# Planned costs, due times and filler products changed in a hand-scheduled recurrence and two gated networks

## The chip, the cores and the metric

The kernel runs on one core of a Trainium2 chip. The metric is the device time of one execution in microseconds; lower is better. Three executions of the kernel before were timed.

## The reference

Three stages follow one another. A linear recurrence over 4 batches and 8 heads (768 positions, head size 48) keeps a 48x48 state for each batch and head; its output, 3072 tokens of 384 values, goes through a first network (d_ff 1536) and then a second (d_ff 2048):

```python
for t in range(S):
    state = alpha[:, :, t, :, None] * state + np.einsum('bhd,bhe->bhde', k[:, :, t], v[:, :, t])
    y[:, :, t] = np.einsum('bhd,bhde->bhe', q[:, :, t], state)
x = y.transpose(0, 2, 1, 3).reshape(B * S, H * D)
x = (x @ w_a) * (x @ w_b) @ w_out                                     # first network
h = x @ w_in
out = (np.maximum(h, 0.0) + alpha2 * np.minimum(h, 0.0)) @ w_out2     # second network
```

The weights arrive as float64; every matrix product is made from a high and a low part of each operand.

## The kernel before

**Work and its tiles.** The 3072 tokens are six blocks (0 to 5) of four chunks each, 24 chunks of 128 positions. A chunk loads `ra` (decay factors), `kq` (keys and queries) and `v` on SyncE's queue; VectorE scans the decays twice (L401, L411) and multiplies them into `kq` (L416); TensorE transposes the keys (`kps`, L452), makes `A` (L470), VectorE masks it to `As` (L479), TensorE makes `y` (L521 and after), and ScalarE and VectorE split `y` into the block's `x` (L605, L609). `A` and `y` of blocks 1 to 5 share one PSUM tile (`pair`), so `A` of a chunk waits until `y` of the chunk before it has been split. The `kq`, `ra` and `v` tiles are rings of two.

**The first network.** Its weights are 18 tiles: six units of `a`, `b` and `o`. Each is loaded as raw 64-bit words (L233) and converted by `conv` on VectorE and ScalarE (six VectorE instructions, L256 to L282). A step is one block with one half unit: nine products into `pa`, nine into `pb`, an elementwise product, and nine products into `acc` two steps later. There are 72 steps in the order of `SEGMENTS`: block 0 with units 0 and 1 (steps 0 to 3), block 1 with units 0 and 1 (steps 4 to 7), the same two blocks with units 2 and 3 and then 4 and 5, and from step 24 on blocks 2 to 5 with all units, 12 steps each. The `pa` and `pb` products keep this order strictly.

**The planner.** No order is written by hand. `Graph.run` is a list scheduler: each operation has an engine, a planned duration, a planned extra latency `lat`, a key and its dependencies; whichever engine can start earliest takes, among its operations that the plan holds ready, the one with the smallest key. The order that results is fixed in each engine's queue, and each engine then runs its queue strictly in that order. Keys are planned nanoseconds. Step k is due at

```python
at = [T_MOE + int(k * 27 * MM * STRETCH) for k in range(len(flat) + LAG + 1)]
```

with MM = 228, and `block_at[n]` is the due time of the first step of block n. A chunk's operations have a key before `block_at[n]`, its loads a key still earlier (`early`); a conversion has the due time of its unit less a lead, its load 15000 less than that. The elementwise operations of a step have keys 40000 before it.

**Filler products.** Where the plan sees TensorE idle by more than PAUSE, `fill` (L176 to L184) puts products of a small constant tile into the queue (`wp`), one for every 110 ns of seven tenths of the planned gap. Their results are used nowhere. They are instructions of the queue: they run whether or not TensorE would in fact have been idle.

**Moves.** In blocks 2 to 5, six small SyncE transfers (L625) bring part of `x` to other partitions before the first `pa` of that block.

Of the kernel before, what the change touches and what calls it, by code (L numbers as in the profile page):

```python
# [23 lines left out]
BC = 4  # L24
# [10 lines left out]

MM = 228
HOP = 250
T_MOE = 32000
STRETCH = 1.22
URGENT = 40000  # L40
PAUSE = 500
SLACK = 1000


class Op:
# [93 lines left out]
def body(tc, akq, v, vg, w_a, w_b, w_o1, w_in, w_o2, beta, out):  # L139
# [13 lines left out]
    with ExitStack() as ctx:  # L153
# [22 lines left out]

        def fill(t0, t1):
            t = mpool.free()
            if t is None or t > t0 + 100:
                return  # L180
            mpool.log.append([])
            wp = ps_mm.tile([P, MB // 2], F32, name="wp", tag="mm")
            for _ in range(int((t1 - t0) * 0.7) // 110):
                nc.tensor.matmul(wp, warm[:, 0:P], warm, start=True, stop=True)  # L184
# [16 lines left out]
        for t in range(KT):  # L201
            for i in range(2):
# [3 lines left out]
                )  # L206

        G = Graph(fill)
        units, uses = {}, {}


        flat = [(n, i, s) for s, (n, u0, u1) in enumerate(SEGMENTS) for i in range(2 * u0, 2 * u1)]
        at = [T_MOE + int(k * 27 * MM * STRETCH) for k in range(len(flat) + LAG + 1)]
        due, block_at = {}, {}
# [8 lines left out]
        def conv(src, tag, name, key, wait, sink, early=15000, on_pe=False, halves=None):  # L223
# [8 lines left out]
                b["raw"] = wpool.tile([P, UC], I64, name=f"r{name}", tag=tags[0])  # L232
                nc.sync.dma_start(b["raw"], src)  # L233

            ld = G.add("SP", 2000, load, key - early, wait, 4000)
            free = cring.take()
            last, highs = [], []
            for n in range(2 if halves else 1):
# [48 lines left out]
                x = G.add("DVE", d(550), sign, key, [m])  # L287
                x = G.add("DVE", d(930), main, key, [x])
                x = G.add("DVE", d(550), power, key, [x])
                x = G.add("DVE", d(930), rest, key, [x])  # L290
                x = G.add("ACT", d(830), high, key, [x], after=highs)
                highs = [x]
                if not on_pe:
                    x = G.add("DVE", d(930), sub, key, [x])
                    x = G.add("DVE", d(930), low, key, [x])
# [26 lines left out]
        def as_unit(r, n):  # L322
            return tuple(y.rearrange("p (t f) -> p t f", t=n) for y in (r[:, 0:UC], r[:, UC : 2 * UC]))

        done, slot_of, taken, loads = {}, {}, {}, {}
        for u in range(NU1):
            for nm, src in (("a", w_a), ("b", w_b), ("o", w_o1)):
                x = nm, u
                slot_of[x] = len(slot_of)
                uses[x] = []  # L330

                def sink(r, x=x):
                    units[x] = as_unit(r, 2 if x[0] == "o" else KT)


                spare = {("a", 0): 3 * NU1 - 1, ("b", 0): 3 * NU1 - 2}.get(x)
                ld, done[x] = conv(src[u], f"w{slot_of[x]}", f"{nm}{u}", due[x] - 20000,
                                   taken.pop(slot_of[x], ()), sink, on_pe=x in ON_PE,
                                   halves=None if spare is None else (f"w{spare}", KT))
                loads[slot_of[x]] = ld  # L340
                if spare is not None:
                    taken[spare] = done[x]
# [4 lines left out]
        xring, lring, rring, vring, zring = Ring(2), Ring(2), Ring(2), Ring(2), Ring(1)  # L347
# [5 lines left out]
        def chunk(g):  # L353
            s = st[g]
            n, c = divmod(g, BC)
            start, moved, end = n == 0, n == 1, n == NB - 1
            key = block_at[n] - (BC - c) * 7500 - 6000 if n else c * 1000 - 100000
            cols = slice(c * CH, (c + 1) * CH)

            def A(eng, dur, fn, deps, early=0, lat=0, after=()):  # L360
                return G.add(eng, dur, fn, key - early, deps, lat, after)
# [3 lines left out]
            if spare is None:  # L365
                rwait, lwait = rring.take(), lring.take()
                rhold, lhold = rring.last(), lring.last()
            else:
                rwait, lwait, rhold, lhold = (), (), [], []
# [22 lines left out]
            kT = lambda: s["kq"][:, 0]  # L392
            qT = lambda: s["kq"][:, 1]
            r0 = lambda: s["ra"][:, 0 : NA - 1].rearrange("p (j t) -> p j t", j=NJ)[:, :, 0:1]
            la = A("SP", 800, load_a, rwait, 14000, 2500)
            lq = A("SP", 1500, load_kq, lwait, 13800, 2500, [la])
            lv = A("SP", 1000, load_v, vring.take(), 12000, 2500)


            def scan_r():  # L400
# [19 lines left out]
            sa = before["scan"] = A("DVE", 1250, scan_a, [rc])  # L420
            slack = SLACK if not start else 0
            k1 = q1 = A("DVE", 1220, mul, [lq, sa], 0, slack)
# [13 lines left out]
            def bank(i):  # L436

                if start:
                    w, accfree[i] = accfree[i], []
                    return (lambda nm: ps_acc.tile([P, NJ, CH], F32, name=nm, tag=f"acc{i}")), w, accfree[i]  # L440
                w = aring.take()
                return (lambda nm: ps_att.tile([P, NJ, CH], F32, name=nm, tag="att")), w, aring.last()
# [5 lines left out]
            if not end:  # L448
# [9 lines left out]
                kbank, w, hold = bank(0)  # L458
                x = A("PE", 480, pe_k, [k1, *w])
# [23 lines left out]
            w = sring.take()  # L483
# [13 lines left out]
            if ks is not None:  # L497
# [8 lines left out]
                w = aring.take()  # L506
# [45 lines left out]
            if moved:  # L552
# [12 lines left out]
                x = A("ACT", 280, ev_3, [py, *yring.take()])  # L565
# [10 lines left out]
            if not end:  # L576
# [7 lines left out]
                x = A("ACT" if start else "DVE", 360, kept, [ds] if start else [ds, zs, py])  # L584
# [46 lines left out]
        for g in range(NG):  # L631
            chunk(g)
# [123 lines left out]
        for k, (n, i, s) in enumerate(flat):  # L756
            u, o = divmod(i, 2)
            x = lambda n=n: xt[n]
# [32 lines left out]
        t0, t1 = block_at[2], block_at[NB - 1]  # L791
        for k in range(2 * NU2):
            b = {}
            key = t0 + k * (t1 - t0) // (2 * NU2)
            _, c = conv((w_in, w_o2)[k % 2][k // 2], f"s{k % 2}", f"s{k % 2}", key,
                        [stored[k - 2]] if k >= 2 else part_users[k], lambda r, b=b: b.update(r=r))

            def store(b=b, k=k):
                nc.sync.dma_start(w2d[k], b["r"].bitcast(F32))

            stored[k] = G.add("SP", 2000, store, key, c, 4000)
# [5 lines left out]
        for k in range(2 * NU2):  # L807
            x = "id"[k % 2], k // 2
# [11 lines left out]
        def load_x2(n):  # L820
            def f():
                xt[NB + n] = xpool.tile([P, 2, NJ, MB], F32R, name="x", tag="x")
                nc.sync.dma_start(xt[NB + n].bitcast(F32)[:, :, 0:KT, :], x2d[n])

            w = xring.take()
            xuse[NB + n] = xring.last()
            return G.add("SP", 4500, f, at2[n * F2] - 30000, [*x2done[n], *w], 4000)
# [25 lines left out]
        for k, (n, i) in enumerate(flat2):  # L853
            if i == 0:
                ld = load_x2(n)
            u, o = divmod(i, 2)
# [98 lines left out]
```

## Time and profile before

| what | value |
|---|---|
| times of three executions | 986.77 us median (986.15 to 987.74) |
| the profiled execution | 986.73 us, span of its instructions 985.0 us |
| TensorE busy | 970.9 us, 99% of the span |
| VectorE busy | 606.5 us, 62% |
| ScalarE busy | 251.9 us, 26% |
| filler products `wp` | 125, from 12.9 to 508.8 us |

The span is what the trace covers; 1.7 us of the execution lie around it. TensorE's busy time counts filler products as work, so a busy TensorE isn't the same as a TensorE that works on the result.

### The profile page before, as it was taken

What the parts mean: (1) busy time and instruction counts of PE and PEld (TensorE: products, weight loads), DVE (VectorE), ACT (ScalarE), POOL (GpSimd) and SP (SyncE); (2) the same over time, 40 slices, a digit from 0 to 9 for tenths busy, and PEclk for the clock granted to TensorE, in tenths of its full rate; (3) what the DMA queues carried; (4) which work ended last, traced back from release to release, by engine and by line L of the source; (5) the groups of instructions that cost most, each with busy time, mean ns of one, the idle gap of its engine ahead of it and who ended that gap; (6) DMA issues with size and microseconds to landing.
All of it is one profiled execution on the core that took longest, in us unless ns stands there. A gap on an engine that the chain in (4) does not pass through costs nothing.

```text
span 985.0 us, 12927 instructions
## 1 busy us (share of the span) xinstructions
PE 970.9 (99%) x5371; PEld 781.6 (79%) x5371; DVE 606.5 (62%) x866; ACT 251.9 (26%) x417; POOL 4.5 (0%) x18
## 2 busy tenths in 40 slices
PE   6999999999999999999999999999999999999998
PEld 5777888878877887788788888888888888888886
DVE  8999988568668867883422245554555555545553
ACT  2443443223323333242122121111111111111111
POOL 1000000000000000000000000000000000000000
PEclk9999999999999999999999999999999999999999
DMA  9952000036345635651045551020110200200000
GB/s 352 394 217 86 1 11 1 13 128 213 124 171 195 239 128 203 195 207 65 33 150 190 191 190 65 1 96 1 47 51 1 86 11 0 96 1 1 33 1 32
DMA packets 30922, 103.92 MB, mean 106 GB/s; under 512 B 3472, under 2 KB 3984, under 8 KB 30864
## 3 DMA queue, kind: packets, MB, share of 16 engines
q1 hardware_dynamic: 30864, 103.11, 29.4%
q8 instruction: 42, 0.69, 0.3%
q14 instruction: 16, 0.13, 0.0%
HBM read 74.78 MB, written 26.74 MB: 103 GB/s over the span
## 4 chain that ended last, share of the span: by engine, by line
PE 98%; DVE 1%; DMA 0%; ACT 0%; issue 0%; DVEq 0%; ACTq 0%
PE acc L641 12%; PE acc L644 12%; PE acc L642 12%; PE pi L641 7%; PE pi L642 7%; PE pi L644 7%; PE pa L641 5%; PE pb L641 5%; PE pa L642 5%; PE pb L642 5%; PE pa L644 5%; PE pb L644 5%; PE A L470 3%; PE y L521 2%; PE wp L184 1%; PE y L527 1%
## 5 line engine op out<-in xcount | busy, mean ns | idle before, releaser
L664 ACT CAST gh<-ng 128x512 fp32r<-128x512 f32 x96 | 59.6, 620 | 328.8 <-DVE ng L867 275.3
L863 DVE TENSOR_SCALAR ng<-pi,betaT 128x512 f32<-128x512 f32 x96 | 72.1, 751 | 106.8 <-PE pi L644 105.9
L668 DVE TENSOR_TENSOR gl<-ng,gh 128x512 fp32r<-128x512 f32 x96 | 66.3, 691 | 79.8 <-ACT gh L664 79.8
L641 PE MATMUL pi<-x,v 128*128 128x512 f32 x288 | 113.3, 393 | 0.0
L644 PE MATMUL acc<-gl,v 128*128 128x512 f32 x288 | 113.0, 392 | 0.0
L642 PE MATMUL pi<-x,v 128*128 128x512 f32 x288 | 112.7, 391 | 0.0
L642 PE MATMUL acc<-gh,v 128*128 128x512 f32 x288 | 112.6, 391 | 0.0
L641 PE MATMUL acc<-gh,v 128*128 128x512 f32 x288 | 112.5, 391 | 0.0
L771 DVE TENSOR_TENSOR a_sb<-a_sb,pb 128x512 f32<-128x512 f32 x72 | 49.4, 686 | 102.0 <-PE pb L644 102.0
L641 PE MATMUL pa<-x,wa 128*128 128x512 f32 x216 | 86.9, 402 | 0.1
L641 PE MATMUL pb<-x,wb 128*128 128x512 f32 x216 | 86.8, 402 | 0.0
L641 PE MATMUL acc<-gh,wo 128*128 128x512 f32 x216 | 86.5, 400 | 0.0
L642 PE MATMUL pa<-x,wa 128*128 128x512 f32 x216 | 84.9, 393 | 0.0
L642 PE MATMUL pb<-x,wb 128*128 128x512 f32 x216 | 84.9, 393 | 0.0
L644 PE MATMUL acc<-gl,wo 128*128 128x512 f32 x216 | 84.9, 393 | 0.0
L642 PE MATMUL acc<-gh,wo 128*128 128x512 f32 x216 | 84.8, 393 | 0.0
L644 PE MATMUL pi<-x,v 128*128 128x512 f32 x288 | 81.5, 391 | 0.0
L664 ACT CAST gh<-a_sb 128x512 fp32r<-128x512 f32 x72 | 44.7, 621 | 143.9 <-DVE a_sb L771 143.4
L768 ACT COPY a_sb<-pa 128x512 f32<-128x512 f32 x72 | 42.2, 587 | 140.9 <-PE pa L644 140.9
L867 DVE SCALAR_TENSOR_TENSOR ng<-pi,ng 128x512 f32<-128x512 f32 x96 | 66.3, 691 | 3.1
L641 PEld LDWEIGHTS pi<-x,v 128*128 128x128 f32 x288 | 54.1, 188 | 13.7 <-DVE ng L867 2.1
L642 PEld LDWEIGHTS acc<-gh,v 128*128 128x128 f32 x288 | 54.1, 188 | 12.2
(107 smaller groups left out, 1441.6 us busy)
## 6 DMA issues: line engine op xcount, KB each, us to landing
kq<-in_akq SPq DMA_DIRECT2D x24, 512.0 KB, 3.7
w2d<-ws SPq DMA_DIRECT2D x16, 768.0 KB, 3.3
v<-w2d SPq DMA_DIRECT2D x16, 768.0 KB, 5.5
x2d<-x SPq DMA_DIRECT2D x18, 512.0 KB, 3.1
x<-x2d SPq DMA_DIRECT2D x6, 1536.0 KB, 6.9
ra<-in_akq SPq DMA_DIRECT2D x24, 258.5 KB, 2.9
v<-in_v SPq DMA_DIRECT2D x24, 256.0 KB, 3.9
rs<-in_w_in SPq DMA_DIRECT2D x8, 768.0 KB, 5.1
```

The costliest lines, as they stand in the source:

```text
L184: nc.tensor.matmul(wp, warm[:, 0:P], warm, start=True, stop=True)
L470: nc.tensor.matmul(A[i][:, j, :], kT()[ps, j, :], qT()[ps, j, :], start=True, stop=True)
L521: nc.tensor.matmul(y_of(j, slice(o, o + 64)), s["v"][:, 2 * j + i, :], s["As"][:, i, j, :], start=first, stop=last)
L641: nc.tensor.matmul(o, lh, rh, start=first and n == 0, stop=False)
L642: nc.tensor.matmul(o, ll, rh, start=False, stop=False)
L644: nc.tensor.matmul(o, lh, rl, start=False, stop=last and n == len(pairs) - 1)
L664: nc.scalar.copy(gq[idx][0], src())
L668: nc.vector.tensor_tensor(out=gl, in0=src(), in1=gh.bitcast(F32), op=ALU.subtract)
L768: nc.scalar.copy(b["a"], ba["t"])
L771: nc.vector.tensor_tensor(out=b["a"], in0=b["a"], in1=bb["t"], op=ALU.mult)
L863: nc.vector.tensor_scalar(out=b["n"], in0=bh["t"], scalar1=0.0, scalar2=betaT[:, i : i + 1], op0=ALU.min, op1=ALU.mult)
L867: nc.vector.scalar_tensor_tensor(out=b["n"], in0=bh["t"], scalar=0.0, in1=b["n"], op0=ALU.max, op1=ALU.add)
```

## The change

Numbers that the planner uses are changed, and one condition is added to `fill`. No instruction's shape or operand is changed; which order the planner then writes follows from the numbers.

```diff
-T_MOE = 32000
-STRETCH = 1.22
+T_MOE = 30000
+STRETCH = 1.2
-SLACK = 1000
+SLACK = 500
...
             t = mpool.free()
-            if t is None or t > t0 + 100:
+            if t is None or t > t0 + 100 or t0 > block_at[2]:
                 return
...
-            ld = G.add("SP", 2000, load, key - early, wait, 4000)
+            ld = G.add("SP", 2100, load, key - early, wait, 4000)
...
-                ld, done[x] = conv(src[u], f"w{slot_of[x]}", f"{nm}{u}", due[x] - 20000,
+                ld, done[x] = conv(src[u], f"w{slot_of[x]}", f"{nm}{u}", due[x] - 18000,
...
-            key = block_at[n] - (BC - c) * 7500 - 6000 if n else c * 1000 - 100000
+            key = block_at[n] - (BC - c) * 9500 - 6000 if n else c * 1000 - 100000
...
-            la = A("SP", 800, load_a, rwait, 14000, 2500)
-            lq = A("SP", 1500, load_kq, lwait, 13800, 2500, [la])
-            lv = A("SP", 1000, load_v, vring.take(), 12000, 2500)
+            la = A("SP", 3200 if g == 0 else 720, load_a, rwait, 14000, 1500 if g == 0 else 3000)
+            lq = A("SP", 1400, load_kq, lwait, 13800, 3000, [la])
+            lv = A("SP", 1250 if start else 720, load_v, vring.take(), 12000, 3000)
```

`SLACK` is extra planned latency, for blocks 1 to 5, behind the multiplication of `kq` and behind the masking of `A`. `start` is true for block 0.

## Rows read from the trace of the kernel before

**Rows 1.** The page: busy time of TensorE; VectorE in 40 slices (tenths).

```profile
PE 970.9 (99%) x5371; PEld 781.6 (79%) x5371; DVE 606.5 (62%) x866; ACT 251.9 (26%) x417; POOL 4.5 (0%) x18
...
DVE  8999988568668867883422245554555555545553
```

**Rows 2.** Chain that ended last, in order of time (start, length): its longest filler pieces.

```profile
67.08 1.53 PE wp L184 x14
...
86.96 2.18 PE wp L184 x19
...
92.65 1.42 PE wp L184 x13
...
506.15 2.96 PE wp L184 x27
```

**Rows 3.** Windows: stretch, busy us (instructions) of each engine, clock, DMA share, GB/s.

```profile
25.00:50.00 25.00, 24.57 (x214) 17.63 (x211) 22.78 (x41) 11.09 (x24) 0.00 (x0) 1.00 1.01 396
```

**Rows 4.** Timeline of VectorE, 0 to 95 us (start, length, instruction, idle before).

```profile
12.06 0.69 DVE L479 TENSOR_TENSOR As<-A,mask 128x512 f32<-128x512 f32 x1 [0.82 <-PE A L470]
...
27.13 1.23 DVE L401 TENSOR_TENSOR_SCAN ra<-ra,ones 128x516 f32<-128x516 f32 x1 [1.23 <-DMA ra<-in_akq]
...
74.87 1.22 DVE L416 TENSOR_TENSOR kq<-kq,ra 128x1024 f32<-128x1024 f32 x1
...
78.15 0.55 DVE L256 TENSOR_SCALAR c<-ra 128x768 uint32<-128x768 uint32 x1
...
81.37 0.61 DVE L609 TENSOR_TENSOR x<-y,x 128x256 fp32r<-128x256 f32 x2
...
86.41 1.22 DVE L479 TENSOR_TENSOR As<-A,mask 128x1024 f32<-128x1024 f32 x1 [0.60 <-PE A L470]
...
91.63 0.93 DVE L279 TENSOR_TENSOR c<-c,wb 128x768 f32<-128x768 f32 x1
...
93.26 0.62 DVE L609 TENSOR_TENSOR x<-y,x 128x256 fp32r<-128x256 f32 x2 [0.43 <-ACT x L605]
```

**Rows 5.** Timeline of TensorE, 0 to 110 us (as rows 4).

```profile
9.88 2.08 PE L470 MATMUL A<-kq 48*128 48x128 f32 x16
...
17.16 1.16 PE L470 MATMUL A<-kq 48*128 48x128 f32 x16
...
82.94 0.48 PE L641 MATMUL acc<-gh,wo 128*128 128x512 f32 x1
...
85.20 1.16 PE L470 MATMUL A<-kq 48*128 48x128 f32 x16
...
89.07 0.44 PE L521 MATMUL y<-As,v 128*64 128x128 f32 x4
...
93.83 0.48 PE L641 MATMUL pa<-x,wa 128*128 128x512 f32 x1
```

**Rows 6.** Timeline of TensorE, 459 to 471 us: the first `y` of block 5.

```profile
459.74 0.39 PE L641 MATMUL pa<-x,wa 128*128 128x512 f32 x1
...
461.89 1.09 PE L521 MATMUL y<-As,v 128*64 128x128 f32 x16
```

**Rows 7.** Timeline of all engines, 495 to 516 us: the entry of block 5.

```profile
502.50 0.69 DVE L609 TENSOR_TENSOR x<-y,x 128x512 fp32r<-128x512 f32 x1 [2.18 <-ACT x L605]
...
503.21 3.87 SPq L625 DMA_DIRECT2D x<-x  x6
...
505.99 3.12 PE L184 MATMUL wp<-ones 128*128 128x256 bf16 x27
...
508.87 0.48 PE L641 MATMUL pa<-x,wa 128*128 128x512 f32 x1
```

**Rows 8.** DMA issues (count, KB each, median us from issue to landing).

```profile
kq<-in_akq SPq DMA_DIRECT2D x24, 512.0 KB, 3.7
...
x<-x SPq DMA_DIRECT2D x24, 64.0 KB, 2.8
```

**Rows 9.** Timeline of SyncE's queue: the load of chunk 4's `ra`.

```profile
18.64 0.38 SPq L379 DMA_DIRECT2D ra<-in_akq  x1
```

## The prediction

> **What bounds the kernel now.** I read the page first. TensorE is busy 99% of the span, VectorE 62%; but VectorE's slices are 8 or 9 for the first five, some 125 us, and 2 to 6 in the second half [rows 1]. So two stages have different limits: up to about 95 us VectorE has more to do than TensorE, afterwards TensorE works without a break. "Without a break" hides one thing: filler products count as work. In the chain of waits, put in order of time, I looked for `wp`: four long pieces, three between 67 and 94 us and one of 27 products at 506 us [rows 2]. The timelines show two short groups, of 0.54 us each, beside those (at 77.8 and 89.8 us), and some more filler ahead of 35 us. Nothing else in the chain after 35 us could be left out: the rest are products that the result needs. So what a new order can win is small: the filler, and the waits of the first 35 us.
>
> Three places, then.
>
> *Start, 0 to 35 us.* Every block-0 chunk hangs on VectorE. It waits 0.82 us at 12.06 for `A` and 1.23 us at 27.13 for chunk 4's `ra` [rows 4], a load that SyncE issued at 18.64 [rows 9]: 8.5 us earlier, while DMA is saturated (share 1.01, 396 GB/s between 25 and 50 us) [rows 3]. VectorE runs in order, so block 0's masks stood behind that scan.
>
> *Entry of block 1, 67 to 94 us.* From 78.15 to 92.56 VectorE fits in eleven instructions of the third units' conversion (first and last in [rows 4]; 4 of 0.55, 6 of 0.95, 1 of 0.93, 8.8 us), which nobody needs before step 8. So here VectorE isn't full: the last chunk is a chain of latencies. Its `kq` is ready at 76.09, the bank is free when the chunk before is split at 81.98 [rows 4], but `A` starts at 85.20, behind a group of nine `acc` products; `As` ends at 87.63 [rows 4] and `y` begins at 89.07 [rows 5], behind 19 filler products. `x` ends at 93.88, step 4 starts at 93.83 by the modelled times.
>
> *Entry of block 5, 506 to 509 us.* Chunk 23's `x` ends at 503.19, the six moves are issued from 503.21 to 507.08, and the first `pa` starts at 508.87 behind 2.88 us of filler [rows 7]. A move takes 2.8 us to land at the median [rows 8], so that `pa` had its data at about the time it started: the filler filled a real wait.
>
> **The change part by part.** All terms are against the profiled execution, 986.73 us, which is the median of the three runs (986.77) to 0.04. A change within 0.2%, 2.0 us, is about what can't be told from none.
>
> *No filler past block 2's due time* concerns the 27 products alone (all others start before 95 us). Taken by itself it is worth 0: the moves set that start. Without its cover TensorE stands idle for those 2.88 us.
>
> *Chunk keys.* Block 5 is due at 482.6 before and 473.2 after; chunk 20 has the key 446.6 and gets 429.2. In the planner's order that means: before, it lies between `pa` of step 55 (445.1) and its `pb` (447.1), and the trace has `y` exactly there, behind a `pa` [rows 6]. After, it lies behind `pa` of step 54 (428.9). That is one step earlier, 27 products at 0.229 us or 6.2 us. Chunks 21 to 23 hang on chunk 20 by the shared bank, so they move along as far as loads and VectorE allow (VectorE's slices there are 2 to 4 [rows 1]). The moves have to be 2.88 us earlier; 6.2 suffice. Value: -2.9 us, bounds 0 and -2.9. Nothing behind it is late next: the second network follows without waits, and its work is the same.
>
> *Block 1.* Its four chunks had the keys 26.0, 33.5, 41.0, 48.5 and get 15.5, 25.0, 34.5, 44.0 (thousands). The second units' `a` and `b` go from 27.0 to 26.8, `o` from 42.0 to 41.8; steps 0 to 2 from 32.0, 39.5, 47.0 to 30.0, 37.4, 44.8. So chunk 5 passes the conversions of `a1` and `b1`, and on TensorE each chunk passes one step more. An earlier chunk chain, with planned latency cut by 500 ns in two places of each chunk, attacks the 67 to 94 us stretch: the five filler groups there take 6.1 us (1.53, 2.18 and 1.42 [rows 2], and the two of 0.54 with the gaps between pieces). In the last chunk alone, 2.3 us lie between the start of the `acc` group and `A`, and 1.4 us between `As` and `y` [rows 4, 5]. Bounds 0 and -6.1; I take the middle, -3.0, since the late part (a bank that must be free, a split that must be done) stays.
>
> *Loads.* The first `ra` is now planned to land at 4.7, `kq` at 7.6; both before came to 3.3 and 4.8. That puts the first multiplication of `kq` ahead of the second scan in the plan, so `A` of chunk 0 comes about one scan (1.2 us) earlier, which covers the 0.82 us. Chunk 4's loads get keys 10.5 earlier and so pass the second units' loads, against the 1.23 us. Bounds 0 and -2.05; I take -1.0.
>
> *What it adds.* Chunk 4 and 5's instructions also stand earlier on VectorE, in front of conversions that TensorE awaits. A load is planned to fly 3.7 us (0.72 + 3.0); in the saturated stretch one took 8.5 us [rows 4, 9], 4.8 us more. Behind a scan that waits stand the masks, splits and conversions, and behind those TensorE. Bounds 0 and +4.8; I take +1.2, a second wait like that of 27.13.
>
> *The rest* (a lead of 18 instead of 20 with T_MOE 30 instead of 32 leaves the first unit's conversions at 12.0; the weight load's 0.1 us; `v`) moves keys by under 1 us up to step 8: 0, hidden by the conversions' own spare time after 95 us.
>
> Sum: -2.9 - 3.0 - 1.0 + 1.2 = -5.7, so 981.0 us.
>
> One more thing could take from it: an idle TensorE can lose its clock. The trace shows both levels: 16 products of `A` took 2.08 us at 9.88, and 1.16 us at 17.16 [rows 5], the lower (1.2 GHz) and the upper one (2.4 GHz); later no fall is seen. The Trainium skill speaks against leaving out filler: "TensorE: Matmul & The Clock Gate", section "Why this matters for your kernels", wants idle gaps between bursts of matmuls kept short, since the clock falls back after one. By that rule the removal would cost here; by the rows, where no gap in mid-kernel is left unfilled, it can't be told. No term above uses it.
>
> **The rivals.**
>
> *Nothing moves at block 1* (the change doesn't do what it says). Said is that the second units' conversions go ahead of block 1's chunks; the keys do the opposite. And 3.7 us is a load's flight over the whole run [rows 8], not where DMA is saturated. If the first 95 us end where they did, only block 5's entry is left: 986.7 - 2.9 = 983.8, and 986.7 if the chain of chunk 23 isn't earlier either. For it: VectorE is near full in the first four slices, and its work is the same. Against: 8.8 us of work that wasn't yet needed.
>
> *VectorE's queue stops at loads in flight* (slower). Place: scans and multiplications of chunks 4 to 6, up to 60 us. Two loads, each late by 4.8 us, cost 9.6 less the 1.2 paid now: 986.7 + 8.4 - 2.9 = 992.2. It decides from 4.9 us of additional waits on, which outweigh block 5's 2.9 and the 2.0 of the measure. For it: the wait at 27.13. Against: the loads are issued earlier too, so less lies ahead of them.
>
> *The clock falls in an unfilled gap.* Place: block 5's entry, if its moves aren't earlier. By [rows 5] the same work takes 0.9 us longer per 1.2 us at the lower level; the start stays low for about 5 us of work, so some 4 us: 990.7. For it: no filler there now. Against: the gap is 2.9 us at most and would probably close.
>
> **How the numbers follow.** Forecast (block 1's entry earlier, block 5's closed) 0.62; nothing moves at block 1 0.23; VectorE's queue stops 0.12; the clock 0.03. The forecast spans all terms at their best, 986.7 - 2.9 - 6.1 - 2.05 = 975.7, to about 984.7, and of the second case the upper end is 986.7. The range 975.5 to 987.0 holds the first two and leaves 0.15 out above. Faster than 984.8: the forecast nearly whole and half of the second case, 0.70; within 0.2%, 0.16; slower than 988.7, 0.14.
>
> **What would show it.** Right: no `wp` after 95 us; the first `pa` of block 5 directly behind `acc` products, with the moves about 6 us further ahead; step 4 at 88 to 91 us and fewer than the third units' eleven instructions on VectorE ahead of it; the first `pa` at about 34 us. All else behind 95 us should be the same distance from its neighbours. Wrong: VectorE waiting on DMA for several us between 25 and 60 us, TensorE idle at `pb` of step 2 because `b1` is late, or products of doubled length after a gap.

## The result and the profile after

The changed kernel takes 977.38 us (median of 4 runs, 976.65 to 977.63), the kernel before 986.83 us in the same measurement: 9.45 us less, a ratio of 0.9902 with a 95% interval of 0.9885 to 0.992. The forecast was 981.0 us, so the direction held and the gain was 1.6 times as large. The profiled execution has a span of 975.8 us against 985.0.

The page of the changed kernel, busy time of TensorE and VectorE's 40 slices:

```profile
PE 962.8 (99%) x5330; PEld 778.1 (80%) x5330; DVE 606.3 (62%) x866; ACT 252.2 (26%) x417; POOL 5.5 (1%) x18
...
DVE  7989888667678867876322254554555555545553
```

VectorE does the same work (606.3 us for 606.5 [rows 1]) and is near full as long as before. TensorE lost 8.1 busy us, of which the 41 filler products that are gone (84 for 125) can be only a part; how much the rest is shows below.

The chain of waits of the changed kernel, in order of time; the longest filler pieces after 35 us, against [rows 2]:

```profile
53.25 1.20 PE wp L184 x10
...
69.12 1.00 PE wp L184 x9
...
89.00 1.97 PE wp L184 x18
```

The last filler product is at 90.7 us: none at block 5, and 4.1 us between step 0 and step 4 for 6.1 before.

The timeline of TensorE at four places (start, length), against [rows 5]:

```profile
7.77 1.08 PE L452 MATMUL kps<-plus,kq 128*128 128x128 f32 x4 [7.77 <-DVE kq L416]
...
16.66 1.16 PE L470 MATMUL A<-kq 48*128 48x128 f32 x16
...
34.20 0.60 PE L452 MATMUL kps<-plus,kq 128*128 128x128 f32 x4
34.73 1.16 PE L470 MATMUL A<-kq 48*128 48x128 f32 x16
35.87 0.67 PE L503 MATMUL dS<-v,ks 128*64 128x48 f32 x16
36.47 0.50 PE L641 MATMUL pa<-x,wa 128*128 128x512 f32 x1
...
88.83 2.13 PE L184 MATMUL wp<-ones 128*128 128x256 bf16 x18
90.72 0.48 PE L641 MATMUL pa<-x,wa 128*128 128x512 f32 x1
```

TensorE's first product starts 1.1 us earlier (8.86 before), yet step 0 comes 1.2 us later (36.47 for 35.27): chunk 4's `kps`, `A` and `dS`, 2.3 us, now stand ahead of it. Step 4 comes at 90.72 for 93.83.

The timeline of all engines around block 5's entry, against [rows 7]:

```profile
489.79 0.69 DVE L609 TENSOR_TENSOR x<-y,x 128x512 fp32r<-128x512 f32 x1 [2.18 <-ACT x L605]
...
490.51 4.61 SPq L625 DMA_DIRECT2D x<-x  x6
...
499.23 0.39 PE L644 MATMUL acc<-gl,wo 128*128 128x512 f32 x1
499.45 0.39 PE L641 MATMUL pa<-x,wa 128*128 128x512 f32 x1
```

The moves start 8.9 us ahead of the first `pa` (5.7 before, 2.9 of it filler), and that `pa` follows the last `acc` product after 0.22 us, the ordinary distance.

Where the 9.2 us between the two profiled executions came from, by the start of the first `pa` of a step in the two timelines:

| stretch | before, us | after, us | difference |
|---|---|---|---|
| start to step 0 | 35.27 | 36.47 | +1.20 |
| step 0 to 4 | 58.56 | 54.25 | -4.31 |
| step 4 to 18 | 84.08 | 82.49 | -1.59 |
| step 18 to 60 | 330.96 | 326.24 | -4.72 |
| step 60 to second network | 70.13 | 70.04 | -0.09 |
| second network to the end | 406.0 | 406.3 | +0.3 |

The first line is the least certain: where the queues up to step 0 are the same, step 0 comes at 35.27 us in the kernel before, 34.91 in e1 and 36.40 in e2 below, while step 0 to 4 takes 58.55 or 58.56 us in each. The third line was in no step of the prediction. Windows of the same length in products, first the kernel before, then the changed one (columns as in [rows 3]):

```profile
93.90:177.80 83.90, 83.90 (x362) 67.98 (x361) 73.47 (x104) 34.12 (x50) 0.00 (x0) 1.00 0.04 14
```

```profile
90.80:173.10 82.30, 82.30 (x362) 67.54 (x361) 72.71 (x102) 35.03 (x51) 0.00 (x0) 1.00 0.04 11
```

362 products fill the window without a gap in both, at the same granted clock of 1.00; they take 83.90 us in one and 82.30 in the other. Counted from start to start, it is 0.2333 us a product against 0.2289. I call that the pace.

### The profile page after: what moved, and what is told of

The parts are those of the page before. It is cut to its first block, busy times and chain, and to the rows that moved or that the text cites. A ratio compares the mean times of both kernels' runs of the same rounds, so it can differ in the third digit from the quotient of the medians.

```text
span 975.8 us, 12828 instructions
## 1 busy us (share of the span) xinstructions
PE 962.8 (99%) x5330; PEld 778.1 (80%) x5330; DVE 606.3 (62%) x866; ACT 252.2 (26%) x417; POOL 5.5 (1%) x18
## 4 chain that ended last, share of the span: by engine, by line
PE 99%; DMA 1%; DVE 0%; ACT 0%; issue 0%; DVEq 0%; ACTq 0%
PE acc L641 12%; PE acc L644 12%; PE acc L642 12%; PE pi L641 7%; PE pi L644 7%; PE pi L642 7%; PE pa L641 5%; PE pb L641 5%; PE pa L642 5%; PE pb L642 5%; PE pa L644 5%; PE pb L644 5%; PE A L470 3%; PE y L521 2%; PE y L527 1%; PE dS L503 1%
```

## The experiments

Two theories stood against each other. The prediction's: the chunks' keys shorten both entries, block 1's and block 5's, and the loads the start. The rival: the keys act at block 5 alone, and SLACK, which the prediction named only beside the keys, shortens block 1's entry. In each run the kernel before was timed on the same chip.

**e1, the kernel before once more.**

> The kernel before once more, unchanged. Between 94 and 187 us its products of 512 columns followed each other every 0.2333 us, after that every 0.2289 us; in the changed kernel they do so every 0.2289 us from 94 us on. If the slower pace belongs to this order of instructions, it stands here again from 94 to 187 us. If it belongs to one execution, the stretch shows 0.229 us and the profiled execution is about 1.6 us shorter (985.1 us instead of 986.7).

Measured: 986.81 us, ratio 1.0003 (0.9994 to 1.0011). Step 4 to step 18 takes 84.09 us again: the slower pace belongs to this program, not to one execution.

**e2, the condition in `fill` alone.**

```diff
-            if t is None or t > t0 + 100:
+            if t is None or t > t0 + 100 or t0 > block_at[2]:
```

> The kernel before with the condition in fill alone: 27 filler products at 506 us go, and every queue keeps its order. The theory of the prediction: the six moves set the first product of block 5, TensorE idles for some 2.9 us and nothing is won, 986.8 us. Rival 1: the filler cost its whole 2.9 us, 983.9 us. Rival 2: the clock falls in the gap, some 4 us, 990.8 us, with products of twice the length behind the gap.

Measured: 986.23 us, ratio 0.9994 (0.9985 to 1.0003): no difference that can be told. Timeline of TensorE at block 5's entry:

```profile
506.88 0.40 PE L644 MATMUL acc<-gl,wo 128*128 128x512 f32 x1
507.65 0.47 PE L641 MATMUL pa<-x,wa 128*128 128x512 f32 x1 [0.38 <-DMA x<-x]
507.96 0.40 PE L642 MATMUL pa<-x,wa 128*128 128x512 f32 x1
508.79 0.47 PE L641 MATMUL pa<-x,wa 128*128 128x512 f32 x1 [0.43 <-DMA x<-x]
509.10 0.40 PE L642 MATMUL pa<-x,wa 128*128 128x512 f32 x1
510.06 0.48 PE L641 MATMUL pa<-x,wa 128*128 128x512 f32 x1 [0.56 <-DMA x<-x]
```

In place of the filler stand three waits for the moves. Against 0.23 us from product to product they cost 0.54, 0.60 and 0.73 us, 1.9 us in all, of the filler's 2.88. So the filler overran by 1.0 us, and the rest was a real wait. The clock holds: the products behind it take 0.40 us as always. In the changed kernel the condition is idle altogether: built without it, every queue is the same, since the plan has no gap there any more that filler would go into.

**e3, the chunks' keys alone.**

```diff
-            key = block_at[n] - (BC - c) * 7500 - 6000 if n else c * 1000 - 100000
+            key = block_at[n] - (BC - c) * 9500 - 6000 if n else c * 1000 - 100000
```

> The kernel before with the chunks' keys alone (9500 for 7500). The prediction had them shorten both entries: block 5 by 2.9 us and block 1 by 3.0, so 980.9 us. Rival: they act at block 5 alone, since the queues of VectorE and TensorE up to about 100 us come out in the same order as before, only some of SyncE's loads are exchanged: 983.9 us, with step 4 at 93.8 us as before.

Measured: 982.70 us, ratio 0.9961 (0.9949 to 0.9974). Timeline of TensorE, first product and entry of step 4:

```profile
9.52 1.09 PE L452 MATMUL kps<-plus,kq 128*128 128x128 f32 x4 [9.52 <-DVE invs L407]
...
93.19 1.58 PE L184 MATMUL wp<-ones 128*128 128x256 bf16 x13
94.53 0.48 PE L641 MATMUL pa<-x,wa 128*128 128x512 f32 x1
```

Step 4 stands 85.0 us behind the first product, and before it was 93.83 - 8.86 = 85.0; step 0 to 4 takes 58.55 us for 58.56: nothing won at block 1. Step 18 to 60 takes 326.7 us for 331.0, 4.3 us less. The rival is right: keys act at block 5, and along the blocks before it. VectorE's queue is the same for its first 237 instructions, up to 180 us, and TensorE's runs just as far.

**e4, SLACK alone.**

```diff
-SLACK = 1000
+SLACK = 500
```

> The kernel before with SLACK 500 for 1000 alone. The prediction named it only beside the keys. If it is what shortens block 1's entry, step 4 comes 2 to 3 us earlier (91 to 92 us); block 5's filler shrinks from 27 to 21 products, so at most 0.7 us more there: 983.5 to 985 us. If the keys or the loads did it, step 4 stays at 93.8 us: 986 us or more.

Measured: 981.66 us, ratio 0.9953 (0.994 to 0.9965), more than either theory had for it. The same rows as for e3:

```profile
8.71 1.09 PE L452 MATMUL kps<-plus,kq 128*128 128x128 f32 x4 [8.71 <-DVE invs L407]
...
89.22 1.58 PE L184 MATMUL wp<-ones 128*128 128x256 bf16 x13
90.56 0.47 PE L641 MATMUL pa<-x,wa 128*128 128x512 f32 x1
```

Step 4 comes 81.9 us behind the first product, 3.1 us earlier, with no other part of the change. `A` of chunk 4 now goes ahead of step 0, at 34.76 us for 37.98, and those of chunks 5 to 7 follow at 51.55, 66.07 and 80.97 us for 55.74, 71.05 and 85.20; the filler between steps 0 and 4 falls from 54 products to 36. From step 18 to 60 SLACK wins a further 2.3 us, all of it between steps 18 and 24, where the keys win 1.8.

**e5, the loads alone** (the four lines of `ld`, `la`, `lq`, `lv` in the diff above).

> The kernel before with the loads' planned durations and flights alone. The prediction had -1.0 us for the start and +1.2 us for scans that wait for loads, so 987.0 us. The keys alone gave -4.2 us and SLACK alone -5.2 us, nearly the whole -9.4 us; if parts add up, the loads are worth about 0: 986 to 988 us, with the first product at 7.8 us instead of 8.9. Rival: the longer planned flights make the plan pad more (141 filler products instead of 125), and it is slower, 988.5 us or more.

Measured: 985.30 us, ratio 0.9982 (0.9973 to 0.999). The first product starts at 7.72 us, step 0 at 34.41 and step 4 at 92.19, 1.6 us earlier than before; step 4 to 18 takes 82.50 us, the faster pace. Behind that, steps 18 to 60 take 331.49 us for 330.95, with nine more filler products at block 5's entry.

**e6, the due times alone.**

```diff
-T_MOE = 32000
-STRETCH = 1.22
+T_MOE = 30000
+STRETCH = 1.2
...
-                ld, done[x] = conv(src[u], f"w{slot_of[x]}", f"{nm}{u}", due[x] - 20000,
+                ld, done[x] = conv(src[u], f"w{slot_of[x]}", f"{nm}{u}", due[x] - 18000,
```

> The kernel before with T_MOE 30000, STRETCH 1.2 and the conversions' lead 18000 alone. The prediction set these to 0: 986.8 us, step 4 at 93.8 us. Rival: earlier due times of the steps shift block 1's entry by themselves, by 2 us either way, 984.8 or 988.8 us.

Measured: 984.95 us, ratio 0.9979 (0.997 to 0.9988). Stretch by stretch it is the kernel before to within 0.4 us, but for one: step 4 to 18 takes 82.49 us for 84.09. Of the 2.1 us by which the profiled execution is shorter, 1.6 are the pace; most of the rest is the start, at 34.87 us for 35.27, and the copy of the kernel before (e1) has 34.91 there.

**e7, the changed kernel with SLACK 1000.**

> The changed kernel with SLACK back at 1000, all else changed. If SLACK is what shortens block 1's entry, some 4 to 5 us of the gain go: 981.5 to 982.5 us, and step 4 stands near 93.8 us. Rival, that keys and loads do it together: 977.4 to 978.4 us.

Measured: 979.09 us, ratio 0.9921 (0.9908 to 0.9933): 1.7 us lost, not 4 to 5. Step 4 is at 92.13, 1.4 us later than in the changed kernel; step 18 to 60 takes 326.65 us, as in the changed kernel, since there the keys alone do it. The interval overlaps that of the changed kernel, so the size of the loss is uncertain.

**e8, the changed kernel with keys 7500.**

> The changed kernel with the chunks' keys back at 7500, all else changed. If the keys act at block 5's entry alone, TensorE waits there again (2 to 3 us, with no filler now) and step 4 stays at 90.7 us: 980 to 981.6 us. Rival, as the prediction had it: block 1's entry goes back too, 983 us or more. If the pace of 0.2333 us hangs on the keys, the stretch behind step 4 shows it again.

Measured: 979.79 us, ratio 0.993 (0.9917 to 0.9942): 2.4 us lost, a little less than expected. Step 4 stays (90.63), the pace stays (82.49 us), and behind step 60's first product the stretch is 2.0 us longer: the wait for the moves again. Here, too, the intervals overlap, at 0.9917 to 0.992.

**e9, the kernel before with one filler product fewer**, 12 for 13 in the last group ahead of step 4.

```diff
+        groups = []
...
+            groups.append(0)
-            for _ in range(int((t1 - t0) * 0.7) // 110):
+            for _ in range(int((t1 - t0) * 0.7) // 110 - (len(groups) == 11)):
```

> The kernel before with one filler product fewer, 12 for 13, in the last group ahead of step 4; every other instruction and every order as before. If the pace behind step 4 (0.2333 or 0.2289 us a product) is a matter of how the first products of that stretch happen to fall, it may show 0.2289 us here: steps 4 to 18 take 82.5 us instead of 84.1, 985.2 us. If it belongs to the order of the chunks and conversions around it, it stays at 0.2333 us: 986.8 us, since step 4 waits for x anyway.

Measured: 985.65 us, ratio 0.999 (0.9981 to 0.9999). Timeline of TensorE at step 4 and a window as above (the line numbers are three higher in this file):

```profile
94.85 1.47 PE L187 MATMUL wp<-ones 128*128 128x256 bf16 x12
96.08 0.48 PE L644 MATMUL pa<-x,wa 128*128 128x512 f32 x1
```

```profile
96.20:178.50 82.30, 82.30 (x362) 67.54 (x361) 73.56 (x105) 34.16 (x50) 0.00 (x0) 1.00 0.04 13
```

The same 362 products in 82.30 us. One product whose result nobody reads, in front of the stretch, decides 1.6 us over the next 84. The medians differ by 0.7 us only; the profiled execution is the slowest of the eleven, with its first product at 9.88 us. Whether the others ran that stretch at the same pace is not shown.

**e10, the changed kernel with no filler at all** (`fill` returns at once).

> The changed kernel with no filler product at all; the order on the other engines is the same, on TensorE all but for the products left out. If filler only covers real waits and the clock holds, 976.5 to 977.4 us. If filler costs its overrun, 974 to 976 us. If TensorE loses its clock in the gaps of the first 90 us, or stays at the lower level longer at the start: products of A at 2.0 us instead of 1.1 beyond 15 us, each chunk 2 us later, 979 to 985 us.

Measured: 974.87 us, ratio 0.9875 (0.986 to 0.989). Timeline of TensorE:

```profile
16.73 2.08 PE L470 MATMUL A<-kq 48*128 48x128 f32 x16
...
24.54 1.80 PE L470 MATMUL A<-kq 48*128 48x128 f32 x16
...
29.49 1.16 PE L470 MATMUL A<-kq 48*128 48x128 f32 x16
...
38.37 0.50 PE L641 MATMUL pa<-x,wa 128*128 128x512 f32 x1
...
89.72 0.50 PE L641 MATMUL pa<-x,wa 128*128 128x512 f32 x1 [0.46 <-ACT x L605]
```

Two opposite effects. At 16.73 the 16 products of `A` still take 2.08 us, at 24.54 1.80, and at 29.49 they take 1.16; with filler they took 1.16 at 16.66 already. So ahead of step 0 the filler gets TensorE to the upper level (2.4 GHz) earlier, and without it step 0 is at 38.37 us, 1.9 us later. From step 0 to 4 it is the reverse: 51.36 us for 54.25, 2.9 us less, though TensorE now waits. That fits filler that overruns, but not all of the 2.9 us need be that: chunk 4's and 5's `A` are 1.9 us late as well, chunk 7's only 0.3, so part can be a late start made good while TensorE would have waited anyway. At step 4 the two leave 1.0 us (89.72 for 90.72), and the profiled execution, the slowest of the four, is 1.0 us shorter in all.

**e11, keys 11500**, and **e12, keys 11500 with SLACK 0**, both on the changed kernel.

```diff
-            key = block_at[n] - (BC - c) * 9500 - 6000 if n else c * 1000 - 100000
+            key = block_at[n] - (BC - c) * 11500 - 6000 if n else c * 1000 - 100000
```

and in e12 also

```diff
-SLACK = 500
+SLACK = 0
```

> The changed kernel with the chunks' keys spread further, 11500 for 9500. The plan then has 8 filler products (0.9 us) between step 0 and step 4 instead of 37 (4.1 us), and 58 instead of 47 ahead of step 0. If the plan's gaps are what block 1's entry costs, 974 to 975 us. If the waits are real and merely not planned, TensorE waits for masks and splits instead, 977 us or more.

> The changed kernel with keys 11500 and SLACK 0: 5 filler products between steps 0 and 4. If less planned latency goes on paying as it did from 1000 to 500, 973 to 975 us. If 500 was about the real extra latency, the order comes too early for the data, TensorE waits in order, and it is 977 us or slower.

Measured: e11 977.31 us, ratio 0.9902 (0.9889 to 0.9916), the changed kernel's own ratio. Its filler between step 0 and 4 falls to 0.9 us as planned, but step 4 comes at 90.41: the waits were real, or came back as later products; which, isn't shown. e12 975.51 us, ratio 0.9884 (0.9871 to 0.9898): step 4 at 88.85. It is below e11, but its interval overlaps that of the changed kernel. e10 is the lowest of all; against e11 on the same chip the intervals only just touch, and against the changed kernel they overlap at 0.9885 to 0.989. A kernel with filler ahead of step 0 alone might keep both halves of e10's finding; it wasn't tried.

## Why the prediction came out as it did

**What bounds the kernel** held: only the stretches up to 95 us and block 5's entry had anything to give in waits.

**Filler at block 5, worth 0 by itself**: right within the measurement (e2), with 1.9 us of real wait under 2.88 us of filler.

**Keys at block 5, -2.9**: right; the gap closed by them alone (e3). Without the filler the moves stood 2.8 us ahead of the first `pa`, now 8.9: 6.1 us more, where one step, 6.2 us, was worked out. The way there was only half as described: `A` of chunk 20 does stand behind `pa` of step 54 now, at 447.88 us, but its `y` follows only at 453.31, and some 4 of the 6.1 us come from the four `y`, which follow every 11.4 us where they came up to 13.4 us apart. In e8, with the old keys and the rest of the change, that distance is 11.4 us as well, and `y` of chunk 20 stands 5.5 us nearer to step 60. What was missed is that the stretch before it gains as well, 1.8 us from step 18 to 60 beyond the filler. The same products are cut up less often: counted in the timelines, runs of 512-column products that end at an attention product are 41 before and 35 after, and each run costs at both ends. One beginning in the timeline of the changed kernel:

```profile
459.25 1.16 PE L470 MATMUL A<-kq 48*128 48x128 f32 x16
460.34 0.50 PE L641 MATMUL acc<-gh,wo 128*128 128x512 f32 x1
460.68 0.39 PE L642 MATMUL acc<-gh,wo 128*128 128x512 f32 x1
460.91 0.40 PE L644 MATMUL acc<-gl,wo 128*128 128x512 f32 x1
```

The first product takes 0.34 us to the next where others take 0.23; the last of a run takes 0.32 or 0.33 before `A`, `dS` or `y`, though 0.23 before `kps`. Six runs fewer, none of them one that ends at `kps`, at 0.21 us are 1.3 of the 1.8 us. Two groups of `kps` have a 512-column product behind them now, which follows after 0.03 us where `A` took 0.20: another 0.3 us. This is worked out from the timelines and not tried by itself.

**Block 1, -3.0**: the size held (step 4 is 3.1 us earlier), the cause didn't. The step that failed is the one that let chunk 5 pass the conversions of `a1` and `b1` by its key. Keys alone leave block 1's entry where it was (e3); SLACK alone moves it by 3.1 us (e4). A key decides only between operations that the plan holds ready at the same time. In this stretch a chunk's next operation is late in the plan because of its planned latency, and that was what SLACK cut: the chunks' `A` took earlier places between the products (e4), and filler shrank. SLACK isn't the only part that acts here: with the loads alone step 4 is at 92.19 us (e5), and at 92.13 with all but SLACK (e7), so that in the changed kernel SLACK adds 1.4 of the 3.1 us. The forecast's -3.0 was the middle of its bounds; that the sum of these parts meets it is luck.

**The start, -1.0**: the first product did come 1.1 us earlier and the wait of 1.23 us is gone, as this timeline of VectorE shows against [rows 4]:

```profile
6.44 1.23 DVE L416 TENSOR_TENSOR kq<-kq,ra 128x1024 f32<-128x1024 f32 x1
...
26.20 1.21 DVE L401 TENSOR_TENSOR_SCAN ra<-ra,ones 128x516 f32<-128x516 f32 x1
```

With the loads changed and SLACK 1000 step 0 is at 34.41 (e5) and 34.46 us (e7); the six executions with neither (the kernel before, e1, e2, e3, e6, e9) have it at 34.87 to 37.58, so there is a gain, but its size isn't sharp. With SLACK 500 it is later instead (36.49 in e4, 36.47 in the changed kernel), because chunk 4's products go ahead of it; that time is given back by step 4.

**Waits for loads, +1.2**: did not occur. VectorE has no wait for DMA between 3.6 and 110 us in the changed kernel. This term stood for a risk and measured 0.

**The rest, 0**: wrong by the pace. The prediction expected everything behind 95 us to keep its distances; step 4 to 18 became 1.6 us shorter. The profile of before showed that stretch at 0.2333 us and all later long ones at 0.2289, but no step of the prediction asked why.

Together: -2.9 and -1.8 (steps 18 to 60), -3.1 (step 4), -1.6 (pace) make -9.4 where -5.7 was forecast; the missing -3.7 are the pace, the fewer runs, and the +1.2 that didn't come, less 0.9 that start and block 1 fell short of -4.0. The range reached down to 975.5 us because all of block 1's filler might go; that 977.38 us lies in it owes something to luck, since 3.4 us came from the pace and the fewer runs, which no term held. Of the signs named, the missing `wp`, the place of the moves, step 4 at 90.72 us and the conversions of the third units on VectorE ahead of it (nine for eleven) came true; step 0 at about 34 us and unchanged distances behind 95 us did not.

**The rivals.** That nothing moves at block 1 and that VectorE's queue stops at loads were both wrong in the outcome, though the keys by themselves do move nothing at block 1 (e3). That the clock falls in the unfilled gap was wrong at block 5: e2 left it unfilled, TensorE waited three times for 0.54 to 0.73 us, and the products behind still took 0.40 us. In e10's start, where bursts have gaps between them, `A` is at the lower level at 16.73 us and at the upper one only at 29.49. The Trainium skill ("TensorE: Matmul & The Clock Gate", section "Why this matters for your kernels") wants TensorE kept busy to get to the upper level, and e10's start agrees.

**The parts don't add up.** Alone they give -0.6, -4.2, -5.2, -1.8 and -2.2 (e2 to e6, medians in the same measurement), together 14.0 us, and the whole gives 9.45. The pace is won once, and loads and due times each contain it; keys and SLACK win the same 2 us in steps 18 to 60. Undone singly, SLACK loses only 1.7 us and the keys 2.4.

## What to carry to other kernels

In a planned order, look first at which planned quantity made an operation late: a key can only choose among operations that the plan already holds ready, and here a planned latency that was too long became real time (e4). Filler products were worth their place where they brought the clock up; where TensorE was already at its upper level, they cost what they overran the real wait by (1.0 us of 2.88 at block 5). Test the two separately. Undo each part of a change as well as trying it alone, because parts that win the same microseconds look like much more when added up.

## What was not expected of the hardware

A gapless stream of 128x512 products ran at one of two paces, 0.2289 or 0.2333 us a product, for 84 us at a time and at the same granted clock. Which one didn't depend on the execution: e1, e2 and e3, whose TensorE queue is that of the kernel before up to there, have the slower pace again, with step 4 at 93.47 to 94.95 us. It could be turned by a single product ahead of the stream (e9, one profiled execution). Of the twelve programs profiled beside the kernel before and the changed one, its copy and e2, e3 and e4 had the slower pace behind step 4, the other eight the faster one. What sets it stays open.
